# Weight conversion in words of 1024 columns, and w3 transposed by VectorE in 32x32 blocks

## The chip, the cores and the metric

The kernel runs on one core of one Trainium2 chip. The metric is the device time of one execution in microseconds (us). An execution takes 872.35 us (median of three, 871.92 to 874.18); the profiled one has a span of 870.7 us from its first to its last instruction. The engines are called TensorE (PE, with its weight loads as PEld), VectorE (DVE), ScalarE (ACT), GpSimd (POOL) and SyncE (SP, which here only issues transfers).

## The reference

An attention block with decay (RetNet, parallel form) is followed by a feed-forward block that multiplies two projections:

```python
scores = scale * np.matmul(q, k.transpose(0, 1, 3, 2))          # q, k, v: (8, 8, 576, 64) fp32
ret = scores * Dmat[None, :, :, :]                              # causal, gamma_h ** (i - j)
x = np.matmul(ret, v).transpose(0, 2, 1, 3).reshape(4608, 512)
a = x @ w1                                                      # w1, w2: 512 x 1024
b = x @ w2
h = a * b @ w3                                                  # w3: 1024 x 1024
out = h @ w_out                                                 # w_out: 1024 x 512
```

The four weight matrices come in as float64, q, k and v as float32; the output is float32, 4608 x 512. So the kernel has to make float32 words from the two 32-bit words of each float64, and it does so with integer and float instructions on the chip.

## The kernel before

**Folding of the last two products.** (a*b) @ w3 @ w_out is computed as (a*b) @ (w3 @ w_out). The small product w3 @ w_out (1024 x 512) is made once on TensorE, called the w3 stage here, and its result is kept in SBUF (`w3o`). For each of the 8 row blocks `ft` of w3 (128 rows), `w3_tr` (L433) transposes the 128 x 1024 block on TensorE in eight 128x128 pieces into PSUM (L438), ScalarE copies them to SBUF (L440) as `w3T`, and `w3_mm` (L443) multiplies the eight pieces with the eight row blocks of w_out into one PSUM bank (L448), which ScalarE copies to `w3o` (L451). A matmul in fp32 appears as two records in the trace.

**The up step.** `up(i, n, fp)` (L476) computes, for a block of tokens (i, n) and a quarter `fp` of the 1024 columns, both x @ w1 and x @ w2 in Strassen form: seven products of four matmuls each (L493) on TensorE, five additions on VectorE (`plus`, L498), two copies on ScalarE (L506, L513), and a last elementwise product a*b (L519). The Strassen sums of the weights (`strassen_weights`, L154, four VectorE instructions, L156) must be made before the ups of that `fp`, and the token sums (`strassen_tokens`, L458) before the ups of that block. `down` (L583) makes the product with `w3o`, also in Strassen form.

**The conversion.** `blocks` (L309) lists the pieces of the weights in the order of use: sixteen of w1 and w2 ("w12", fp, j, r), eight of w_out ("wo", g), and sixteen of w3 ("w3", ft, g0). Each is 128 x 512 float64, 512 KB. `load_block` (L319) issues the transfer of the next one on SyncE's queue, into one of five `raw` buffers. The conversion of a block is five VectorE and two ScalarE instructions:

- `begin_block` (L353): the exponent `e` from the high word (L362), the mantissa `m` from the high word (L366), the low word added to the mantissa (L369), and on ScalarE two ReLUs that clamp and shift the exponent (L372, L373);
- `end_block` (L378): the sign put into `e` (L383), the last reader of `raw`, and the final product m * e (L392), which writes to the place of use: `wA`, `wo`, or a row block `w3`. When a block is done, the next transfer is issued.

**What sets the order.** Instructions are issued in the order of the program text, and each engine takes its own in that order. The conversion is a generator that stops (yields) after each VectorE instruction, and `convert(n)` (L422) lets it go n steps. `plus` calls `convert(conv)` after each addition, so the steps of the conversion lie between the additions of the ups: `conv=2` with another two at the end of each up while w1 and w2 are converted, less after that. In the w3 stage a loop (L730) takes the six ups that are left one by one, transposes and multiplies w3 row blocks as they are ready, and calls `convert(10)` between row blocks once the ups are used up. A row block of w3 isn't finished before the one two ahead of it has been turned (`turned`, L387).

PSUM has seven banks in rotation for all products (`acc`). The memory on the right side of SBUF holds first the attention's buffers beside `raw`, and from L722 on `ab3`, `wst` (w3, w3T, wo) beside `raw`; when these are closed (L748, L760) it holds attention's buffers again, for the chunks of tokens from number `NC` on, whose transfers are then issued (L762).

The function that the change removes is this:

```python
    def w3_tr(ft):
        t = pools["wst"].tile([P, KF, P], F32, tag="w3T", name="w3T")
        for i in range(0, KF, NP):
            tp = acc.tile([P, NP, P], F32, tag="acc", name="tp")
            for n in range(NP):
                nc.tensor.transpose(tp[:, n, :], live["w3", ft][:, (i + n) * P:(i + n + 1) * P],
                                    ident)
            nc.scalar.copy(t[:, i:i + NP, :], tp)
        live["w3T", ft] = t
```

Of the kernel before, what the change touches and what calls it, by code (L numbers as in the profile page):

```python
# [8 lines left out]
F32 = mybir.dt.float32  # L9
I32 = mybir.dt.int32  # L10
U32 = mybir.dt.uint32
ALU = mybir.AluOpType
PSUM = bass.MemoryType.PSUM

# [24 lines left out]
def kernel(  # L39
# [13 lines left out]
    nc = tc.nc  # L53
# [5 lines left out]
    CV = 512  # L59
# [15 lines left out]
    QC = CV // 2  # L75
# [65 lines left out]

    halves = range(DF // CV)
    wA = [wp.tile([P, 2, KD, CV], F32, tag=f"wA{h}", name="wA") for h in halves]
# [10 lines left out]
    def strassen_weights(fp):  # L154
        def tt(out, in0, in1, op):
            nc.vector.tensor_tensor(out=A(fp, out), in0=A(fp, in0), in1=A(fp, in1), op=op)  # L156

        tt("S1", "A21", "A22", ALU.add)
        tt("S2", "S1", "A11", ALU.subtract)
        yield  # L160
        tt("S3", "A11", "A21", ALU.subtract)
        tt("S4", "A12", "S2", ALU.subtract)
        live["S", fp] = True
        yield

    BL = 32
# [142 lines left out]
    blocks = []  # L309
    for fp in range(NQ):  # L310
        for j, w in enumerate((moe_w1, moe_w2)):
            for r in range(2):
                blocks.append((("w12", fp, j, r), w))
    blocks += [(("wo", g), moe_w_out) for g in range(KF)]
    blocks += [(("w3", ft, g0), moe_w3) for ft in range(KF) for g0 in range(0, DF, CV)]
    at = {key: n for n, (key, _) in enumerate(blocks)}
    loaded, begun, converted, turned = [0], [0], [0], [0]

    def load_block():  # L319
        n = loaded[0]  # L320
        if n == len(blocks):
            return
        key, w = blocks[n]
        t = raw.tile([P, CV, 2], I32, tag="raw", name="raw", bufs=5)
        if key[0] == "w12":
            _, fp, _, r = key
            src = w[2 * r * P:2 * (r + 1) * P, fp * QC:(fp + 1) * QC, :]
            t2 = t.rearrange("p (c n) t -> p c n t", c=2)
            if r == 0:
                nc.sync.dma_start(t2, src.rearrange("(c p) n t -> p c n t", p=P))  # L330
            else:
                for half in range(2):
                    nc.sync.dma_start(t2[heads[half]],
                                      src.rearrange("(c a d) n t -> a d c n t", a=2, d=D)[1 - half])
        else:
            r, c0 = (key[1], 0) if key[0] == "wo" else key[1:]
            nc.sync.dma_start(t, w[r * P:(r + 1) * P, c0:c0 + CV, :])
        live["raw", n] = t
        loaded[0] += 1

    def converted_to(n):
        key, _ = blocks[n]
        if key[0] == "w12":
            _, fp, j, r = key
            return wA[fp // 2][:, j, 2 * r:2 * r + 2, fp % 2 * QC:fp % 2 * QC + QC]
        if key[0] == "wo":
            return live["wo"][:, key[1], :]
        _, ft, g0 = key
        if ("w3", ft) not in live:
            live["w3", ft] = pools["wst"].tile([P, DF], F32, tag="w3", name="w3")  # L350
        return live["w3", ft][:, g0:g0 + CV]

    def begin_block():  # L353
        n = begun[0]
        t = live["raw", n]
        lo, hi = t[:, :, 0], t[:, :, 1]
        e = raw.tile([P, CV], I32, tag="exp", name="e")
        m = raw.tile([P, CV], I32, tag="man", name="m")
        vec = nc.vector


        vec.tensor_scalar(out=e, in0=hi, scalar1=1, scalar2=21,  # L362
                          op0=ALU.logical_shift_left, op1=ALU.logical_shift_right)
        yield

        vec.tensor_scalar(out=m, in0=hi, scalar1=0x000FFFFF, scalar2=0x00100000,  # L366
                          op0=ALU.bitwise_and, op1=ALU.bitwise_or)
        yield
        vec.scalar_tensor_tensor(m.bitcast(F32), in0=lo.bitcast(U32), scalar=2.0 ** -32, in1=m,  # L369
                                 op0=ALU.mult, op1=ALU.add)  # L370
        relu = mybir.ActivationFunctionType.Relu
        nc.scalar.activation(e, e, relu, bias=lim[:, 0:1], scale=-1.0)  # L372
        nc.scalar.activation(e, e, relu, bias=lim[:, 1:2], scale=-2.0 ** 23)  # L373
        live["em", n] = e, m
        begun[0] += 1
        yield

    def end_block():  # L378
        n = converted[0]
        hi = live["raw", n][:, :, 1]  # L380
        e, m = live["em", n]
        vec = nc.vector
        vec.scalar_tensor_tensor(e, in0=hi, scalar=-(1 << 31), in1=e,  # L383
                                 op0=ALU.bitwise_and, op1=ALU.bitwise_or)
        yield
        key = blocks[n][0]
        while not (key[0] == "w12" or "wo" in live and (key[0] == "wo" or key[1] < turned[0] + 2)):  # L387
            yield "wait"
        out, m, e = converted_to(n), m.bitcast(F32), e.bitcast(F32)
        if key[0] == "w12":  # L390
            m, e = (x.rearrange("p (c n) -> p c n", c=2) for x in (m, e))
        vec.scalar_tensor_tensor(out, in0=m, scalar=2.0 ** -20, in1=e, op0=ALU.mult, op1=ALU.mult)  # L392
        converted[0] += 1

        if n >= 4:
            load_block()
        if key[0] == "w12" and key[1] > 0 and key[2:] == (1, 1):
            yield from strassen_weights(key[1])
        yield

    def conversion():


        yield from begin_block()
        while converted[0] < len(blocks):
            if begun[0] < len(blocks) and converted[0] not in (1, 2, 3):
                yield from begin_block()
            yield from end_block()
            if begun[0] == converted[0] < len(blocks):
                yield from begin_block()  # L410
# [11 lines left out]
    def convert(n):  # L422

        for _ in range(n):
            if go_on() is not None:
                return

    def convert_up_to(n):
        while converted[0] < n:
            assert go_on() is None  # L430


    def w3_tr(ft):  # L433
        t = pools["wst"].tile([P, KF, P], F32, tag="w3T", name="w3T")
        for i in range(0, KF, NP):
            tp = acc.tile([P, NP, P], F32, tag="acc", name="tp")
            for n in range(NP):
                nc.tensor.transpose(tp[:, n, :], live["w3", ft][:, (i + n) * P:(i + n + 1) * P],  # L438
                                    ident)
            nc.scalar.copy(t[:, i:i + NP, :], tp)  # L440
        live["w3T", ft] = t

    def w3_mm(ft, part):  # L443
        if part == 0:
            live["w3ps"] = acc.tile([P, DM], F32, tag="acc", name="ps")
        ps = live["w3ps"]
        for g in range(part * NP, part * NP + NP):
            nc.tensor.matmul(ps, live["w3T", ft][:, g, :], live["wo"][:, g, :],  # L448
                             start=(g == 0), stop=(g == KF - 1))
        if part == 1:  # L450
            nc.scalar.copy(live["w3o"][:, ft, :], ps)  # L451
# [24 lines left out]
    def up(i, n, fp, conv=0, tail=True):  # L476
# [43 lines left out]
        if tail:  # L520
            convert(conv)
# [142 lines left out]
    load_block()  # L664
# [8 lines left out]
    convert_up_to(3)  # L673
    load_block()
# [11 lines left out]
    up(0, 0, 0, conv=2, tail=False)  # L686
# [4 lines left out]
    convert(2)  # L691
# [4 lines left out]
    convert(5)  # L696
# [7 lines left out]
    up(0, 0, 1, conv=2)  # L704
# [5 lines left out]
    up(0, 1, 0, conv=2)  # L710
    pv(4)
    up(0, 1, 1, conv=2)
    up(0, 0, 2, conv=2)
# [11 lines left out]
    pools["forms"] = ctx.enter_context(tc.tile_pool(name="forms", bufs=1, reuse_waits="tile"))  # L725
# [3 lines left out]
    multiplied = 0  # L729
    while multiplied < KF:  # L730
        if todo:
            first = converted[0] < 4 * NQ
            up(*todo.pop(0), conv=2 if first else 1)
            convert(0 if first else 3)
        ft = multiplied
        begun_ft = ft < turned[0]
        if begun_ft:
            w3_mm(ft, 0)
        if turned[0] < KF and (not todo or converted[0] > at["w3", turned[0], DF - CV]):
            convert_up_to(at["w3", turned[0], DF - CV] + 1)  # L740
            w3_tr(turned[0])
            turned[0] += 1
        if begun_ft:
            w3_mm(ft, 1)
            multiplied += 1
        if not todo:
            convert(10)
# [3 lines left out]
    for nm in ("wB", "carry", "ot"):  # L751
        pools[nm] = ctx.enter_context(tc.tile_pool(name=nm, bufs=1, reuse_waits="tile"))
    xps.append(ctx.enter_context(tc.tile_pool(name="xp1", bufs=1, reuse_waits="tile")))
# [6 lines left out]
    weights_part.close()  # L760
    open_attention(ctx)
# [124 lines left out]
```

## Time and profile before

| what | value |
|---|---|
| time, median of three | 872.35 us |
| TensorE busy | 851.9 us, 98% of the span |
| VectorE busy | 458.3 us, 53% |
| ScalarE busy | 194.7 us, 22% |
| GpSimd busy | 111.8 us, 13% |
| up products on the chain that ended last (L493) | 46% |
| down products on it (L599) | 25% |
| w3 products on it (L448) | 6% |
| w3 transposes on it (L438) | 1% |

The busy share of an engine is an average over the whole span. TensorE's granted clock was full in nearly all of it. By stretches of the span, the busy times in us are:

| stretch, us | TensorE | VectorE | ScalarE | GB/s moved |
|---|---|---|---|---|
| 0 to 33.8 (first chunks, first weights) | 21.4 | 18.4 | 16.4 | 204 |
| 33.8 to 120.8 (ups with w1, w2 conversion) | 86.2 | 81.3 | 47.0 | 144 |
| 120.8 to 165.35 (ups with w_out, w3 conversion) | 43.2 | 39.8 | 17.9 | 107 |
| 165.35 to 222.7 (w3 stage) | 57.4 | 31.8 | 26.4 | 115 |
| 222.7 to 870.7 (all the rest) | 643.8 | 287.0 | 87.0 | 50 |

A group of instructions in the profile is shown as line, engine, operation, output <- inputs, shapes and count, then busy us and mean ns of one, then the idle time of the engine just before them and what ended it. A wait is shown as engine, what waited, what it waited for, and then us in total, times and the longest. The duration of one instruction includes a start that can overlap with the instruction before it; how far apart the starts lie is read from the timeline.

### The profile page before, as it was taken

What the parts mean: (1) busy time and instruction counts of PE and PEld (TensorE: products, weight loads), DVE (VectorE), ACT (ScalarE), POOL (GpSimd) and SP (SyncE); (2) the same over time, 40 slices, a digit from 0 to 9 for tenths busy, and PEclk for the clock granted to TensorE, in tenths of its full rate; (3) what the DMA queues carried; (4) which work ended last, traced back from release to release, by engine and by line L of the source; (5) the groups of instructions that cost most, each with busy time, mean ns of one, the idle gap of its engine ahead of it and who ended that gap; (6) DMA issues with size and microseconds to landing.
All of it is one profiled execution on the core that took longest, in us unless ns stands there. A gap on an engine that the chain in (4) does not pass through costs nothing.

```text
span 870.7 us, 15305 instructions
## 1 busy us (share of the span) xinstructions
PE 851.9 (98%) x6373; PEld 779.0 (89%) x6373; DVE 458.3 (53%) x781; ACT 194.7 (22%) x390; POOL 111.8 (13%) x91
## 2 busy tenths in 40 slices
PE   5899999999999999999999999999999999999998
PEld 5899999645888999999999999999999999999996
DVE  4799998973543344643544544534543434334343
ACT  3676333553022221101111101111101100001000
POOL 3000020002001323201212030230300101000000
PEclk9999999999999999999999999999999999999999
DMA  9993443437035444515242335061300000000001
GB/s 194 218 223 107 98 99 104 139 120 108 1 77 118 114 63 82 95 28 93 49 84 44 55 68 96 27 104 34 59 25 25 2 25 1 25 24 1 25 1 49
DMA packets 187332, 63.20 MB, mean 73 GB/s; under 512 B 175480, under 2 KB 175480, under 8 KB 187264
## 3 DMA queue, kind: packets, MB, share of 16 engines
q1 hardware_dynamic: 154624, 54.07, 29.2%
q10 hardware_dynamic: 32640, 8.16, 4.9%
q8 instruction: 50, 0.82, 0.4%
q14 instruction: 18, 0.15, 0.1%
HBM read 52.76 MB, written 9.44 MB: 71 GB/s over the span
## 4 chain that ended last, share of the span: by engine, by line
PE 88%; DVE 3%; issue 1%; DMA 1%; ACT 1%; DVEq 0%; ACTq 0%; SPq 0%
PE up L493 46%; PE po L599 25%; PE ps L448 6%; PE sc L241 4%; PE xps L298 3%; PE xps L291 2%; PE tp L226 1%; PE st L263 1%; DVE c L498 1%; PE tp L438 1%; DVE e L383 0%; DMA raw<-in_moe_w_dram 0%; ACT e L372 0%; DVE ab L519 0%; DVE w L392 0%
## 5 line engine op out<-in xcount | busy, mean ns | idle before, releaser
L498 DVE TENSOR_TENSOR c<-up,c 128x384 f32<-128x384 f32 x240 | 133.2, 555 | 198.0 <-PE up L493 193.2
L493 PE MATMUL up<-xT,wA 128*128 128x192 f32 x1152 | 213.5, 329 | 1.0 <-ACT xT L303 1.0
L493 PEld LDWEIGHTS up<-xT,wA 128*128 128x128 f32 x1152 | 191.9, 191 | 3.6 <-ACT xT L303 1.2
L493 PE MATMUL up<-T,wS 128*128 128x192 f32 x768 | 141.1, 327 | 2.1 <-DVE T L467 2.1
L493 PEld LDWEIGHTS up<-T,wS 128*128 128x128 f32 x768 | 127.8, 191 | 2.4 <-issue 2.4
L599 PE MATMUL po<-w3o,ab 128*128 128x256 f32 x456 | 104.2, 381 | 0.3 <-ACT ot L621 0.3
L599 PEld LDWEIGHTS po<-w3o,ab 128*128 128x128 f32 x456 | 86.0, 190 | 12.1 <-ACT ot L621 0.7
L603 DVE TENSOR_TENSOR ot<-po,ot 128x256 f32<-128x256 f32 x90 | 38.1, 424 | 72.3 <-PE po L599 70.6
L513 ACT COPY c<-up 128x384 f32<-128x384 f32 x48 | 22.9, 477 | 226.3 <-PE up L493 222.0
L493 PE MATMUL up<-xT,wS 128*128 128x192 f32 x384 | 70.6, 327 | 0.6 <-DVE c L498 0.5
L493 PE MATMUL up<-T,wA 128*128 128x192 f32 x384 | 70.3, 326 | 0.0
L244 DVE TENSOR_TENSOR pm<-sc,mask 128x512 f32<-128x512 f32 (+1 forms) x80 | 45.5, 628 | 46.7 <-PE sc L241 46.5
L599 PE MATMUL po<-wB,forms 128*128 128x256 f32 x288 | 65.1, 379 | 0.0
L493 PEld LDWEIGHTS up<-xT,wS 128*128 128x128 f32 x384 | 63.6, 190 | 1.5 <-DVE c L498 1.5
L493 PEld LDWEIGHTS up<-T,wA 128*128 128x128 f32 x384 | 63.7, 190 | 0.0
L599 PEld LDWEIGHTS po<-wB,forms 128*128 128x128 f32 x288 | 54.8, 190 | 7.3
L212 POOL TENSOR_TENSOR ld_v<-ld_v,gk 128x1024 f32<-128x1024 f32 (+1 forms) x17 | 32.3, 1900 | 213.6 <-DMA ld_v<-in_v_dram 186.3
L448 PE MATMUL ps<-wo,w3T 128*128 128x512 f32 x128 | 56.4, 593 | 0.2 <-ACT w3T L440 0.2
L506 ACT COPY c<-up 128x384 f32<-128x384 f32 x48 | 22.8, 476 | 117.4 <-PE up L493 68.4
L467 POOL TENSOR_TENSOR T<-xT,T 128x384 f32<-128x384 f32 x20 | 20.9, 1043 | 217.1 <-PE up L493 215.4
L519 DVE TENSOR_TENSOR ab<-c 128x768 f32<-128x768 f32 x48 | 46.6, 972 | 3.8
L448 PEld LDWEIGHTS ps<-wo,w3T 128*128 128x128 f32 x128 | 23.7, 190 | 27.2 <-issue 26.7
(75 smaller groups left out, 817.8 us busy)
## 6 DMA issues: line engine op xcount, KB each, us to landing
raw<-in_moe_w_dram SPq DMA_DIRECT2D x24, 512.0 KB, 3.7
out_dram<-ot SPq DMA_DIRECT2D x24, 256.0 KB, 2.0
bl_q<-in_q_dram SPq DMA_DIRECT2D x136, 32.0 KB, 2.1
bl_k<-in_k_dram SPq DMA_DIRECT2D x136, 32.0 KB, 2.2
raw<-in_moe_w_dram SPq DMA_DIRECT2D x16, 256.0 KB, 6.1
ld_k<-in_k_dram SPq DMA_DIRECT2D x8, 512.0 KB, 7.1
ld_q<-in_q_dram SPq DMA_DIRECT2D x8, 512.0 KB, 8.2
ld_v<-in_v_dram SPq DMA_DIRECT2D x8, 512.0 KB, 7.4
```

Of the source, the lines that this page charges most:

```text
L212: nc.gpsimd.tensor_tensor(out=t, in0=t, in1=gam[:sz, c].unsqueeze(1).unsqueeze(3).to_broadcast([sz, 2, H, D]), op=ALU.mult)
L241: nc.tensor.matmul(sc[j][:sz, p, :sz], kT[hs, b, p, :sz], qT[hs, b, p, :sz], start=True, stop=True)
L244: nc.vector.tensor_mul(pm[:sz, b, j, :, :sz], sc[j][:sz, :, :sz], mask[:sz, :sz].unsqueeze(1).to_broadcast([sz, NP, sz]))
L298: nc.tensor.matmul(banks[r][heads[half], b, n, :sz], vs[:sz, b * H + 2 * p + j, :], pm[:sz, b, j, p, :sz], start=(c == 0 and m == 0), stop ...
L448: nc.tensor.matmul(ps, live["w3T", ft][:, g, :], live["wo"][:, g, :], start=(g == 0), stop=(g == KF - 1))
L493: nc.tensor.matmul(ps[:, w, :], a[:, w, r, :], b[:, r, :], start=(new and w == r == 0), stop=(w == r == 1), skip_group_check=True)
L498: nc.vector.tensor_add(c[:, to], ps, c[:, sb])
L506: nc.scalar.copy(c[:, 0], p1)
L513: nc.scalar.copy(c[:, 0], p1)
L519: nc.vector.tensor_mul(ab[:, 4 * fp:4 * fp + 4, :], c[:, :, 0, :], c[:, :, 1, :])
L599: nc.tensor.matmul(ps[nm], a[A][:, f, :], live["W"][B][:, f, :], start=(f == 0 and not on), stop=(f == NP - 1), skip_group_check=True)
L603: nc.vector.tensor_add(ot[:, to[0], to[1]], ps[nm], ot[:, sb[0], sb[1]])
```

## The change

The conversion works on 1024 columns at a time: one item is two of the former blocks, a transfer of 1 MB in three buffers of twice the size, an exponent buffer of twice the width, and one mantissa buffer in place of two. The two first items (w1 and w2 of fp = 0) are still loaded and converted in halves of 512. The order of steps within an item changes: the exponent of the next item is begun between the mantissa of an item and its sign.

The rows of w3 are no longer transposed on TensorE. Four transfers bring 32-row blocks of a row block of w3 to four groups of 32 partitions, so that a VectorE transpose, which exchanges rows and columns within 32x32 blocks, gives the whole `w3T`. The inner dimension is then taken in another order (a, i, x), and w_out is loaded in the same order. It takes away `w3_tr`, the PSUM banks and the ScalarE copies of the transposes. `w3_mm` makes its eight matmuls in one go.

The pace of the conversion is set anew for items of double width (conv=1 where it was 2), and two pools are opened later: `forms` after the w3 stage, and `xp1` after the conversion's memory is closed.

```diff
-    CV = 512
+    CV = 1024
+    HC = CV // 2
...
+    blocks = [("w12", fp, j) for fp in range(NQ) for j in range(2)]
+    blocks += [("wo", g, 0) for g in range(0, KF, 2)]
+    blocks += [("w3", ft, 0) for ft in range(KF)]
+
+    items = []
+    for key in blocks:
+        items += [(key, h * HC, HC) for h in range(2)] if key[:2] == ("w12", 0) else [(key, 0, CV)]
...
-        t = raw.tile([P, CV, 2], I32, tag="raw", name="raw", bufs=5)
...
+            live["raw", key] = raw.tile([P, CV, 2], I32, tag="raw", name="raw", bufs=3)
...
+        elif kind == "wo":
+            src = moe_w_out.rearrange("(a i x) n t -> i a x n t", i=KF, x=BL)
+            t4 = t.rearrange("p (c n) t -> p c n t", c=2)
+            for c in range(2):
+                nc.sync.dma_start(t4[:, c], src[r + c])
         else:
-            r, c0 = (key[1], 0) if key[0] == "wo" else key[1:]
-            nc.sync.dma_start(t, w[r * P:(r + 1) * P, c0:c0 + CV, :])
-        live["raw", n] = t
+            src = moe_w3[r * P:(r + 1) * P].rearrange("(j r) (a f) t -> a r j f t", r=BL, f=FA)
+            t4 = t.rearrange("p (j f) t -> p j f t", f=FA)
+            for a in range(P // BL):
+                nc.sync.dma_start(t4[a * BL:(a + 1) * BL], src[a])
         loaded[0] += 1
...
+            live["m", key] = raw.tile([P, CV], I32, tag="man", name="m", bufs=1)
...
-        while not (key[0] == "w12" or "wo" in live and (key[0] == "wo" or key[1] < turned[0] + 2)):
+        while not (kind == "w12" or "wo" in live and (kind == "wo" or r < multiplied[0] + 2)):
             yield "wait"
...
+            flat = pools["wst"].tile([P, CV], F32, tag="w3", name="w3", bufs=1)
+            out = flat.rearrange("p (c n) -> p c n", n=QC)
...
+        if kind == "w3":
+            yield
+            t = pools["wst"].tile([P, KF, P], F32, tag="w3T", name="w3T")
+            vec.transpose(t.rearrange("p i (j r) -> p j i r", r=BL), flat)
+            live["w3T", r] = t
         converted[0] += 1
...
-        yield from begin_block()
-        while converted[0] < len(blocks):
-            if begun[0] < len(blocks) and converted[0] not in (1, 2, 3):
-                yield from begin_block()
-            yield from end_block()
-            if begun[0] == converted[0] < len(blocks):
-                yield from begin_block()
+        while converted[0] < len(items):
+            if begun[0] == converted[0]:
+                yield from begin_item()
+            yield from mantissas()
+            if converted[0] >= 4 and begun[0] < len(items):
+                yield from begin_item()
+            yield from end_item()
...
-    def w3_tr(ft):
-        t = pools["wst"].tile([P, KF, P], F32, tag="w3T", name="w3T")
-        for i in range(0, KF, NP):
-            tp = acc.tile([P, NP, P], F32, tag="acc", name="tp")
-            for n in range(NP):
-                nc.tensor.transpose(tp[:, n, :], live["w3", ft][:, (i + n) * P:(i + n + 1) * P],
-                                    ident)
-            nc.scalar.copy(t[:, i:i + NP, :], tp)
-        live["w3T", ft] = t
-
-    def w3_mm(ft, part):
-        if part == 0:
-            live["w3ps"] = acc.tile([P, DM], F32, tag="acc", name="ps")
-        ps = live["w3ps"]
-        for g in range(part * NP, part * NP + NP):
+    multiplied = [0]
+
+    def w3_mm(ft):
+        ps = acc.tile([P, DM], F32, tag="acc", name="ps")
+        for g in range(KF):
             nc.tensor.matmul(ps, live["w3T", ft][:, g, :], live["wo"][:, g, :],
                              start=(g == 0), stop=(g == KF - 1))
-        if part == 1:
-            nc.scalar.copy(live["w3o"][:, ft, :], ps)
+        nc.scalar.copy(live["w3o"][:, ft, :], ps)
+        multiplied[0] += 1
...
-    up(0, 0, 0, conv=2, tail=False)
+    up(0, 0, 0, conv=1)
     front(2)
     convert(1)
     scale(3, "q")
     front(3, "k")
-    convert(2)
     score(2)
     state(2)
     scale(3, "v", True)
     front(3, "q")
-    convert(5)
+    convert(3)
     pv(2)
...
-    up(0, 1, 1, conv=2)
-    up(0, 0, 2, conv=2)
+    up(0, 1, 1, conv=1, tail=1)
+    up(0, 0, 2, conv=1, tail=1)
...
-    while multiplied < KF:
+    while multiplied[0] < KF:
+        ft = multiplied[0]
         if todo:
-            first = converted[0] < 4 * NQ
-            up(*todo.pop(0), conv=2 if first else 1)
-            convert(0 if first else 3)
...
+            up(*todo.pop(0), conv=1, tail=converted[0] < at["wo", 0, 0])
+        else:
+            convert_up_to(at["w3", ft, 0] + 1)
+        if converted[0] > at["w3", ft, 0]:
+            w3_mm(ft)
+            convert(1 if todo else 6)
     w3_part.close()
...
-    for nm in ("wB", "carry", "ot"):
+    for nm in ("forms", "wB", "carry", "ot"):
         pools[nm] = ctx.enter_context(tc.tile_pool(name=nm, bufs=1, reuse_waits="tile"))
-    xps.append(ctx.enter_context(tc.tile_pool(name="xp1", bufs=1, reuse_waits="tile")))
...
     weights_part.close()
+    xps.append(ctx.enter_context(tc.tile_pool(name="xp1", bufs=1, reuse_waits="tile")))
     open_attention(ctx)
```

## The prediction

> **What bounds the kernel now.** I read the page's busy shares and slices first, then TensorE's waits, then the chain around the w3 stage, then the durations.
>
> ```profile
> PE 851.9 (98%) x6373; PEld 779.0 (89%) x6373; DVE 458.3 (53%) x781; ACT 194.7 (22%) x390; POOL 111.8 (13%) x91
> ...
> PE   5899999999999999999999999999999999999998
> ...
> DVE  4799998973543344643544544534543434334343
> ```
>
> A slice is 21.8 us. TensorE is the bound almost everywhere, so a microsecond of its work removed is a microsecond gained. VectorE is at 90% or more in slices 2 to 5 and again in slice 7, where the weights are converted: there it is a second limit just under the first. TensorE's waits on others (us in total, times, longest) show how close:
>
> ```profile
> PE up L493 <- DVE T L467: 2.1, 1, 2.1
> PE tp L438 <- DVE w L392: 1.1, 1, 1.1
> PE up L493 <- DVE c L498: 0.5, 1, 0.5
> PE ps L448 <- ACT w3T L440: 0.2, 1, 0.2
> ```
>
> The first ends at 33.8 us, in the start-up, and the change doesn't touch what it waits for. The others, with a short gap of about 0.2 us at 120.6, are 0.53 + 0.2 + 0.24 + 1.14 = 2.1 us that TensorE loses between 33.8 and 222.7 us because conversion is late. The chain of waits in order of time (start, us) at the w3 stage:
>
> ```profile
> 163.88 0.61 DVE e L383
> 164.51 0.70 DVE w L392
> 165.35 0.63 PE tp L438 x4
> 165.98 6.87 PE ps L448 x16
> 172.84 0.88 PE tp L438 x8
> 173.72 6.87 PE ps L448 x16
> 180.59 0.87 PE tp L438 x8
> ```
>
> From 165.4 to 222.7 us TensorE never pauses: each row block of w3 takes 6.87 us of products (an fp32 matmul is two records here, so x16 is 8 of them) and 0.875 us of eight transposes. Durations by form:
>
> ```profile
> L438 PE MATMUL tp<-ident,w 128*128 128x128 f32 x64 | 8.5, 273 | 1.1 <-DVE w L392 1.1
> L440 ACT COPY w3T<-tp 128x512 f32<-128x512 f32 x16 | 8.6, 587 | 5.9 <-PE tp L438 5.8
> L372 ACT ACTIVATE e<-e,lim 128x512 int32<-128x512 int32 x40 | 28.9, 723 | 44.3 <-DVE e L362 44.2
> L369 DVE SCALAR_TENSOR_TENSOR m<-raw,m 128x512 f32<-128x512 uint32 x40 | 27.6, 690 | 0.9
> L362 DVE TENSOR_SCALAR e<-raw 128x512 int32<-128x512 int32 x40 | 18.2, 456 | 4.1 <-DMA raw<-in_moe_w_dram 3.5
> L198 DVE STREAM_TRANSPOSE kT<-bl_k 128x1024 f32<-128x1024 f32 x8 | 9.9, 1239 | 0.0
> L536 DVE TENSOR_TENSOR w3o<-w3o 128x1024 f32<-128x1024 f32 x1 | 1.2, 1214 | 0.0
> ```
>
> 273 ns overstates what a transpose takes from TensorE, since neighbours overlap: eight pass in 0.875 us, 0.109 us each.
>
> [...]
>
> **The change, part by part.**
>
> *TensorE's transposes go.* 8 row blocks x 8 x 0.109 us = 7.0 us, all on TensorE's continuous path: -7.0.
>
> *VectorE transposes.* Eight 128x1024 at 1.24 us each (the L198 row) = 9.9 us added. Off TensorE's path if VectorE keeps up, which the next items examine. ScalarE loses 16 x 0.587 = 9.4 us of copies.
>
> *Words of 1024 instead of pairs of 512.* In the timeline, independent VectorE instructions start 0.33 us (TENSOR_SCALAR) and 0.60 us (SCALAR_TENSOR_TENSOR) after one another at 512; a dependent one waits for the full 0.69. The stream part doubles, the rest doesn't: 512 more elements add 0.53 us (1214 against 683 in the tensor_tensor rows) or half of it, 0.27. So 0.60 and 1.14 at 1024. A pair of blocks cost 2 x (2 x 0.33 + 3 x 0.60) = 4.9 us; a 1024-item costs 2 x 0.60 + 3 x 1.14 = 4.6. Eighteen such items save 5.4 us. Net for VectorE: +4.5 us over some 190 us.
>
> *The pace.* Before, an up step of 9.1 us on TensorE carries about 12 conversion steps: 12 x 0.49 + 5 additions x 0.47 + one product of 0.87 = 9.1 us of VectorE, equal to TensorE's, and anything extra (four Strassen sums, GpSimd beside it) makes it late. After, an up carries at most 6 steps. Following the generator by hand, the VectorE load of the ups from (0,0,1) on is 7.4 to 9.1 us each, mostly 7.8, and in the last, (0,2,2), the first w3 block's transpose is issued ahead of the last addition, some 0.2 us before the products want it. So the 2.1 us of lateness goes: -2.1.
>
> *One new wait at the second product.* In the order of issue, behind up(0,2,2)'s last matmul VectorE still has: addition 0.5, m 0.6, product 0.87, then for block 1 mantissa 1.2, next exponent 0.6, sign 1.14, final 1.22, transpose 1.24: 7.4 us, against 6.87 of w3_mm(0). TensorE waits 0.6; the ends are 0 (VectorE less behind) and 1.5 (every instruction at its dependent duration). I take +0.6.
>
> *The steady w3 stage.* VectorE needs 1.14 + 0.60 + 1.14 + 1.22 + 1.24 + 0.60 = 5.9 us per block, under 6.87. A longer loop runs through ScalarE: the ReLUs of block f+2 stand in its queue behind the copy of product f, which waits for TensorE. From the start of product f: 6.87 + copy 0.59 + two ReLUs + sign 1.22 + final 1.22 + transpose 1.24, to be ready when product f+2 starts, 13.74 later. No trace row has a 1024-wide ReLU: the lower end by slope (the trace's copies: 1048 ns at 1024, so about 0.43 per 512) is 1.16, the upper end twice 0.723 = 1.45. With 1.16 the sum is 13.5, hidden with 0.2 us to spare; with 1.45 and everything dependent 14.5, late by 0.8 every second block, 2.3 us in all. I take 0, as the wait at product 1 gives 0.6 us more room.
>
> *1 MB items in three buffers.* Where before an exponent step needed 512 KB, it needs 1 MB. In the first 70 us the transfers run at some 215 GB/s and limit. The item ("w12", 2, 0) is begun while (1,1) is still unfinished, so the sums of fp=1 stand behind it on VectorE. Its second half is the old block issued at 46.9 and 47.7 us, landing 6.2 to 6.5 us later: 54.1. By my count VectorE gets there at about 52. Then e 0.6, sign and final 2.3, S1 and S2 1.4 put S2 at 58.5, while TensorE wants it at 57.7 for the second product of up(0,0,1): +0.8, ends 0 and 1.8. The earlier items land in time: (1,1)'s last part at 41.5, wanted at 41.3. Later stages move 107 GB/s or so with a whole up of lead: hidden. The first 33.8 us keep their order, since the first four items stay 512 wide.
>
> *Placement.* forms and xp1 are opened later, raw grows by 4 KB and e/m by 4 KB in a partition. The last raw buffer comes free some 10 us before up(0,2,3) begins instead of 18, and the q/k/v loads that reuse it have more than 20 us until they are wanted: zero, hidden by up(0,2,3) and the first down.
>
> Sum: 872.35 - 7.0 - 2.1 + 0.6 + 0.8 = 864.7.
>
> **Rivals.** (1) *The ReLU loop or the product-1 wait is at its upper end*: +0.9 and +2.3 over the forecast, 867.9 with both. For: 0.2 us of room, and VectorE waits for ReLUs now (L383 sat idle 8.3 us for them). Against: ScalarE loses its w3T copies. (2) *Data late in the first 70 us*: +1.0 at S2 and a VectorE that stays late until up(0,1,0), which keeps the 0.5 and 0.2 us waits: 866.5; if the score and transposes of the next chunk are also late by 2 us, 868.5. For: transfers limit there. Against: VectorE has less to do in each later up. (3) *VectorE becomes the bound, slower*: beside GpSimd the trace shows exponents at 1.10 and signs at 1.02 instead of 0.42 and 0.69. If wide instructions ran at 1.4 times my price throughout, a w3 block takes 8.3 us instead of 6.87 (seven gaps, +10), and the ups at 10.2 instead of 9.1 add about 1.1 x 3: 864.7 + 13 = 878. Against: GpSimd is idle in the records between 130 and 200 us, and the 1024-wide rows at hand show no such price. (4) *The gain is eaten exactly*: 871 to 873, from (1) and (2) together with half of (3).
>
> **How the numbers follow.** Forecast 0.68; rival 1 0.12; rival 2 0.08; rival 3 0.07; rival 4 0.05. The low end is the forecast without both new waits and a little more: 864.7 - 0.6 - 0.8 - 0.7 = 862.6. The high end takes in (1) and (2): 869.5. Faster by over 0.3% means under 869.7: forecast, (1), nearly all of (2): 0.86. Within 0.3%: 0.07. Slower: 0.07.
>
> **What would show it.** Right: no tp line in the w3 stage; eight ps stretches at 6.87 us spacing but for a wait of about 0.6 us ahead of the second, on the VectorE transpose; up(0,2,3) starting near 215 instead of 222.7; TensorE's waits on c and w gone; a wait on wS of under 1 us near 58; VectorE's 1024-wide rows near 1.2 and 0.7, its transposes near 1.24, ReLUs near 1.16; after the w3 stage everything as before, only earlier. Wrong: ps spacing over 7.2 us with ScalarE's e or VectorE's transpose as what ends the wait; VectorE's load per up above 9.1; a wait on raw transfers of more than 2 us after 33 us; or a changed front before 33.8 us.

## The result and the profile after

The kernel became **slower**: 884.66 us (median of 4 runs, 884.39 to 885.97) against 872.84 us for the kernel before on the same chip (4 runs). The ratio is 1.0137, with an interval of 1.012 to 1.0155. The forecast was 864.7 with an upper end of 869.5, so both the sign and the range were wrong.

The page of the changed kernel begins as follows (busy time and share of each engine; then the span in 40 slices of 22.1 us, with TensorE's granted clock in tenths):

```profile
span 882.3 us, 15042 instructions
...
PE 849.8 (96%) x6309; PEld 773.9 (88%) x6309; DVE 460.3 (52%) x699; ACT 176.6 (20%) x338; POOL 112.4 (13%) x91
...
PE   5898995999999999999999999999999999999998
...
DVE  4896884898444333644544534444543424434243
...
PEclk9999998899999999999999999999999999999999
```

TensorE has 2.1 us less to do (851.9 before), although 7.0 us of transposes left it: the matmuls that remain took longer in places. It is idle for 882.3 - 849.8 = 32.5 us, before for 870.7 - 851.9 = 18.8. The holes are in slices 4 and 7, counted from one (about 66 to 88 and 132 to 154 us; the prediction counted its slices from zero), and in and after the second the clock falls too (mean over the span 0.990, before 0.998). The kernel isn't slower everywhere; it has two bad places. Four landmarks on TensorE divide the time (us):

| stretch | before | after | difference |
|---|---|---|---|
| start to up(0,1,1) | 84.58 | 90.43 | +5.85 |
| from there to the start of the w3 stage (its first transpose before, its first product after) | 74.2 | 86.3 | +12.1 |
| from there to up(0,2,3), the w3 stage | 63.94 | 56.70 | -7.2 |
| the rest | 647.97 | 648.84 | +0.9 |

The third row is the gain that was forecast. In the kernel before it counts from 158.8 us, where the first transposes begin; the earlier table counted the w3 stage from 165.35, the end of TensorE's last pause in it. The waits of TensorE in the first 250 us name the others (us in total, times, longest):

```profile
PE up L513 <- DVE c L518: 10.6, 2, 9.3
...
PE tp L227 <- POOL ld_q L213: 2.2, 2, 1.4
PE tp L227 <- ACT ld_q L211: 2.1, 3, 1.6
PE sc L242 <- ACT qT L230: 2.1, 1, 2.1
```

`c <- up` (L518) is the addition of an up, which frees a PSUM bank. It is not an expensive instruction (0.55 us), so the question is what stood ahead of it on VectorE. The chain of waits, 132 to 155 us (start, us), answers:

```profile
132.72 0.69 DVE e L369
133.41 0.33 SPq L349
...
133.78 18.10 DMA raw<-in_moe_w_out_dram
...
151.98 0.06 DVE e L369
...
152.59 0.55 DVE c L518
...
154.19 0.56 DVE c L518
```

The last item of w_out was on its way for **18.1 us**. VectorE had the exponent step `e` of this item (L369) at the head of its queue and waited 10.5 us for the data; the additions behind it could not pass. One of them reads the bank into which TensorE's next product adds, so TensorE waited too. Its timeline (start, us; in brackets the wait ahead of it) shows the price twice:

```profile
144.06 1.46 PE L513 MATMUL up<-xT,wA 128*128 128x192 f32 x8
154.79 2.93 PE L513 MATMUL up<-xT,wS 128*128 128x192 f32 x8 [9.27 <-DVE c L518]
157.51 2.35 PE L513 MATMUL up<-xT,wA 128*128 128x192 f32 x8
159.70 1.46 PE L513 MATMUL up<-T,wS 128*128 128x192 f32 x8
```

After 9.27 us of waiting the same eight records took 2.93 and 2.35 us, where they take 1.46 undisturbed: (2.93 - 1.46) + (2.35 - 1.46) = 2.4 us more. The granted clock was 0.50 from 150 to 158 us and 1.00 from 160 on. 9.3 + 2.4 is nearly the whole +12.1 of the second row.

**Why 18.1 us?** A window by window view (length, then busy time of TensorE, its loads, VectorE, ScalarE and GpSimd, granted clock, share of the 16 DMA engines in use, GB/s), first while only w_out is under way, then beside w3's first transfers (asked for from 135.0 us on), then with w_out alone again, and after TensorE's restart:

```profile
92.00:96.00 4.00, 4.00 (x27) 4.00 (x26) 2.36 (x5) 0.45 (x1) 0.00 (x0) 1.00 0.25 100
...
138.00:140.00 2.00, 2.00 (x14) 2.00 (x13) 2.00 (x3) 0.00 (x0) 0.00 (x0) 1.00 1.08 131
...
148.00:152.00 4.00, 0.00 (x0) 0.00 (x0) 0.02 (x1) 0.00 (x0) 0.00 (x0) 0.63 0.26 95
...
154.00:156.00 2.00, 1.21 (x4) 1.21 (x5) 2.00 (x4) 1.40 (x2) 0.00 (x0) 0.50 0.26 61
```

With w_out alone the share is 0.25, which is 4 of 16 engines, and 100 GB/s are moved. At that rate 1 MB takes 10.5 us (an estimate from this row); the rest of the 18.1 us went by while w3's transfers were under way beside it. In the kernel before, 512 KB of w_out landed in 3.5 us, 150 GB/s:

```profile
raw<-in_moe_w_out_dram SPq DMA_DIRECT2D x8, 512.0 KB, 3.5
```

The source of the changed transfer, `(a i x) n t -> i a x n t`, has a = 4 as its outermost dimension. In the kernel before it is the 128 rows, and with w_out alone under way from 92 to 96 us the share there is 0.54, with 177 GB/s moved. That the 4 is what holds the share at 0.25 is a reading of these two traces; experiments 1 and 4 test it.

**Why was it asked for so late?** The transfers' issues on SyncE's queue, of the changed kernel and then of the one before (start, time taken):

```profile
86.72 25.12 SPq L349 DMA_DIRECT2D raw<-in_moe_w_out_dram  x6
111.89 21.18 SPq L736 DMA_DIRECT2D gqs<-decay_q_dram  x16
133.18 1.14 SPq L349 DMA_DIRECT2D raw<-in_moe_w_out_dram  x2
```

```profile
102.54 10.51 SPq L721 DMA_DIRECT2D gqs<-decay_q_dram  x16
```

Sixteen small transfers (2.2 KB each) stand between the third item of w_out and the fourth. They took 21.18 us to issue behind the four-engine transfers, 10.51 before, and the last item of w_out was asked for only at 133.2. Small as they are, they keep the DMA engines in use: from 128 to 132 us the share was 0.60 with 4 GB/s moved. VectorE wanted the item at 141.5, 8.3 us after it was asked for. At the 150 GB/s of before, 1 MB would take 7.0 us (an estimate from the row above).

**The first row.** The chain of waits, 65 to 79 us, of the changed kernel:

```profile
65.93 0.61 DVE e L369
...
66.57 1.16 ACT e L372
...
67.75 1.15 ACT e L373
68.90 2.35 ACT ld_q L211 x8
...
71.29 1.33 PE tp L227 x5
72.62 1.70 PE xps L292 x32
...
78.20 1.82 PE up L513 x10
```

In the kernel before, ScalarE's timeline has a ReLU of half the width and the same scaling of q here (start, us, line):

```profile
61.90 0.72 ACT L372 ACTIVATE e<-e,lim 128x512 int32<-128x512 int32 x1 [3.49 <-DVE e L362]
...
63.43 2.46 ACT L210 ACTIVATE ld_q<-ld_q,gq 128x128 f32<-128x128 f32 x8
```

ScalarE's scaling of q for chunk 4 (L211), which the next transposes need, is put in its queue by hand after the fourth addition of up(0,0,1). Two ReLUs stand ahead of it in both kernels. Now each takes 1.15 us where it was 0.72, and their input, the exponent step on VectorE, comes 4.5 us later than before (65.93 against 61.45): the new order puts the mantissa steps of an item ahead of the next item's exponent, and up(0,0,1) itself begins 1.4 us later. So q is scaled from 68.9 us on instead of 63.4, and more of this comes from the late input than from the length of the ReLUs. TensorE waits 2.1 us and then runs at a lower clock (0.51 granted from 72 to 74 us): the 32 products of L292 take 1.70 us, in the kernel before 1.03. It reaches up(0,1,0) at 78.20, before at 72.36. An earlier wait of 2.1 us on qT, near 46 us, has the same form: copies behind ReLUs. It is where the 1.4 us at the start of up(0,0,1) come from, out of the row's 5.85.

**What was forecast and came.** The chain in the w3 stage has nothing left but products (a stretch of x64 is 4 row blocks), and the rows by form have the forecast durations:

```profile
184.38 27.96 PE ps L468 x64
...
219.46 14.00 PE ps L468 x32
233.46 2.61 PE up L513 x16
```

```profile
L390 DVE SCALAR_TENSOR_TENSOR m<-raw,m 128x1024 f32<-128x1024 uint32 x18 | 22.4, 1242 | 0.2
L372 ACT ACTIVATE e<-e,lim 128x1024 int32<-128x1024 int32 x18 | 20.7, 1150 | 38.5 <-DVE e L369 38.5
L369 DVE TENSOR_SCALAR e<-raw 128x1024 int32<-128x1024 int32 x18 | 12.5, 693 | 13.2 <-DMA raw<-in_moe_w_out_dram 10.5 <-DMA raw<-in_moe_w_dram 2.7
L420 DVE STREAM_TRANSPOSE w3T<-w 128x1024 f32<-128x1024 f32 x8 | 9.9, 1244 | 1.0 <-DVE w L416 0.5
```

The third row holds the cause in its last columns: of 13.2 us idle ahead of `e`, 10.5 were for w_out.

### The profile page after: what moved, and what is told of

Its sections match the earlier page's. It is cut to its first block, busy times and chain, and to the rows that moved or that the text cites. A ratio compares the mean times of both kernels' runs of the same rounds, so it can differ in the third digit from the quotient of the medians.

```text
span 882.3 us, 15042 instructions
## 1 busy us (share of the span) xinstructions
PE 849.8 (96%) x6309; PEld 773.9 (88%) x6309; DVE 460.3 (52%) x699; ACT 176.6 (20%) x338; POOL 112.4 (13%) x91
## 4 chain that ended last, share of the span: by engine, by line
PE 83%; DVE 6%; DMA 6%; issue 2%; ACT 1%; SPq 0%; POOL 0%; DVEq 0%; ACTq 0%; POOLq 0%
PE up L513 44%; PE po L618 24%; PE ps L468 5%; PE sc L242 3%; PE xps L299 3%; DMA raw<-in_moe_w_out_dram 2%; DMA raw<-in_moe_w_dram 2%; PE xps L292 2%; PE tp L227 1%; DVE c L518 1%; PE st L264 1%; DMA ld_q<-in_q_dram 1%; DMA ld_k<-in_k_dram 1%; DVE e L401 1%; DVE wS L159 1%
## 5 line engine op out<-in xcount | busy, mean ns | idle before, releaser
L518 DVE TENSOR_TENSOR c<-up,c 128x384 f32<-128x384 f32 x240 | 133.3, 555 | 190.8 <-PE up L513 183.3
L618 PEld LDWEIGHTS po<-w3o,ab 128*128 128x128 f32 x456 | 85.8, 190 | 13.2 <-DVE ab L584 0.9
```

Of the source, the lines that this page charges most:

```text
L518: nc.vector.tensor_add(c[:, to], ps, c[:, sb])
L618: nc.tensor.matmul(ps[nm], a[A][:, f, :], live["W"][B][:, f, :], start=(f == 0 and not on), stop=(f == NP - 1), skip_group_check=True)
```

## The experiments

The theory was: two independent losses, (A) w_out on four engines, asked for late, and (B) ScalarE's order in the first 90 us. Rivals were: words of 1024 make VectorE or ScalarE late everywhere; the order of SyncE alone is to blame; the w3 stage doesn't pay. Ratios are to the kernel before on the same chip, with intervals; diffs without another name are against the changed kernel.

**1. w_out in pieces of 32 partitions.** The data are the same, but each transfer has 32 as its outermost dimension.

```diff
             for c in range(2):
-                nc.sync.dma_start(t4[:, c], src[r + c])
+                for a in range(P // BL):
+                    nc.sync.dma_start(t4[a * BL:(a + 1) * BL, c], src[r + c][a])
```

> The changed kernel with each w_out transfer of 128 partitions split into four of 32 partitions; addresses and bytes are the same. Theory (the outermost dimension of 4 confines a w_out transfer to 4 of the 16 DMA engines): a 1 MB item lands in under 8 us instead of 18, TensorE's 9.3 us wait and the slow clock behind it go, 871 to 874 us. Rival (the scattered rows of w_out in memory are slow, or the transfers behind them are): landing stays near 18 us and the time near 884.7.

Measured: 873.14 us, ratio 1.0004 (0.9996 to 1.0013). The wait of 9.3 us on `c` is gone (1.3 remains, at 119 us), the sixteen small transfers take 8.56 us to issue, and in the window that follows the first issues the engines are in use three times as much:

```profile
88.00:92.00 4.00, 4.00 (x72) 3.43 (x71) 3.40 (x5) 1.57 (x4) 0.00 (x0) 1.00 0.78 200
```

The changed kernel has 0.27 and 78 GB/s there. The addresses are the same, so it was not where w_out's rows lie in memory; what differs is the outermost dimension of each transfer, 32 instead of 4. So (A) cost 1.3% of the time, nearly all of the loss.

**2. The small transfers later.** w_out stays on four engines, but the sixteen transfers of gqs are moved behind the w3 stage.

```diff
-    for a in range(2):
-        for f in range(D // BL):
...
     keep_stores.clear()
     store()
+    for a in range(2):
+        for f in range(D // BL):
...
```

> The changed kernel with the sixteen small gqs transfers issued after the w3 stage instead of ahead of the last w_out item. Theory (4 engines for w_out, and the queue that the gqs transfers hold up): the last w_out item is issued near 125.5 instead of 133.2 and lands near 143.7; VectorE's wait falls from 10.5 us to about 2, TensorE's from 9.3 to at most 1.5: 873 to 877 us. Rival (only the issue time matters, or only the rate): no wait at all and the same time as with the split transfers, or an unchanged 884.7.

Measured: 874.19 us, ratio 1.0016 (1.0007 to 1.0024). The last item of w_out is asked for at 126.7 us instead of 133.2, and VectorE's wait for it shrinks from 10.5 us to 1.9:

```profile
DVE e L369 <- DMA raw<-in_moe_w_out_dram: 1.9, 1, 1.9
```

TensorE's waits on `c` come to 2.0 us. Either repair is nearly enough: in the changed kernel the low rate did its harm only together with the late issue.

**3. Scaling q one addition earlier.** Only (B) is touched.

```diff
-    aside.extend([lambda: None] * 3 + [lambda: scale(4, "q", True)])
+    aside.extend([lambda: None] * 2 + [lambda: scale(4, "q", True)])
```

> The changed kernel with ScalarE's scaling of q of chunk 4 placed one addition earlier in up(0,0,1), ahead of the two wide ReLUs instead of behind them. Theory (ScalarE's order costs the first 90 us): TensorE's 2.1 us of waits on ld_q near 69 us and the slow clock after them go; up(0,1,0) starts near 74 instead of 78.1; the w_out wait stays, unless the later start shortens it: 880 to 882 us. Rival (q arrives late over the DMA, or VectorE is late): up(0,1,0) still starts near 78 and the time stays at 884.7.

Measured: 880.9 us, ratio 1.0094 (1.0074 to 1.0115). up(0,1,0) starts at 73.77 instead of 78.20, and up(0,1,1) at 86.00 instead of 90.43; the wait at w_out stays at 9.2 us. So the place of one instruction group in ScalarE's queue was worth 0.4%.

**4. The kernel before, with w_out on four engines.** This puts (A) into the kernel before, without any other part of the change. The rows of w_out are then paired with other columns of w3 than in the reference, so the folded product is another one; the work is the same.

```diff
-            r, c0 = (key[1], 0) if key[0] == "wo" else key[1:]
-            nc.sync.dma_start(t, w[r * P:(r + 1) * P, c0:c0 + CV, :])
+            if key[0] == "wo":
+                src = w.rearrange("(a i x) n t -> i a x n t", i=KF, x=32)[key[1]]
...
+            nc.sync.dma_start(t, src)
```

> The kernel before, with w_out alone loaded in rows (a, i, x) as in the change, 512 KB in one transfer with an outermost dimension of 4; rows of w_out are then paired with other columns of w3, so the folded product is not the reference's. Theory (4 engines): such a transfer takes some 9 us instead of 3.5, eight of them 72 us from 81.5 on, where 50 us are at hand: 885 to 895 us with waits on raw<-in_moe_w_out_dram. Rival (the rate of w_out matters only with 1 MB items and three buffers): 872 to 875.

Measured: 879.12 us, ratio 1.008 (1.0062 to 1.0098), less than expected. In the chain an item of 512 KB is on its way for 9.6 us, with two more items and the last of the small transfers asked for around it:

```profile
120.78 9.61 DMA raw<-in_moe_w_out_dram
```

TensorE waits 3.1 us instead of 9.3, then the clock is low (0.57 from 132 to 140 us). The expectation let eight transfers of 9 us follow one another, about half of the 18.1 us that 1 MB had taken beside w3's transfers. Where w_out alone is under way, from 92 to 104 us, the trace shows 86 to 103 GB/s at a share of 0.23 to 0.26; at that rate 512 KB take 5 to 6 us (an estimate). The access order therefore costs 6 to 7 us before the change, 11.6 after it.

**5. Experiments 1 and 3 together.**

> The changed kernel with both edits together: w_out in transfers of 32 partitions, and the scaling of q ahead of the wide ReLUs. Theory (two separate causes, the 16 engines and ScalarE's order): the gains add, 884.7 - 11.5 - 3.8 = 869.4, so 868 to 871. Rival (the same slack was spent twice): 872 to 873.

Measured: 867.96 us, ratio 0.994 (0.9925 to 0.9954). From 67 to 86 us the chain now has no hole (the wait on qT near 46 us stays):

```profile
67.43 1.75 PE tp L227 x16
...
74.10 9.30 PE up L514 x56
83.39 1.03 PE xps L292 x32
```

(1.33 + 0.43)% was the sum of the two alone, 1.97% is what both bring, so the two losses are independent to within the intervals, and repaired, the change is a gain.

**6. and 11. The pace of the conversion.** What remained in 5 was a wait of 1.8 us on qT, one of 1.3 on `c`, and 0.6 on wS. Experiment 6 moves conversion steps from the end of up(0,0,0) to a place behind front(2), and within up(0,1,2) from the first two additions to the third and fourth; 11 does only the first.

```diff
-    up(0, 0, 0, conv=1)
+    up(0, 0, 0, conv=[1, 1, 1, 0, 0])
...
+    convert(2)
     score(2)
...
-            up(*todo.pop(0), conv=1, tail=converted[0] < at["wo", 0, 0])
+            pace = [0, 0, 2, 2, 1] if len(todo) == 6 else 1
+            up(*todo.pop(0), conv=pace, tail=converted[0] < at["wo", 0, 0])
```

> As the one before, and the pace mended at two places: in up(0,0,0) the exponent step of the second 1 MB item comes after front(2), so that ScalarE makes c and the copies of kT and qT first; in up(0,1,2) the Strassen sums of fp = 3 come after the third addition, which frees the bank p5 that the seventh product writes. Theory: the 1.3 us wait of sc on qT and the 1.3 us wait of up on c go, with some slow clock behind the first: 865.5 to 868. Rival (VectorE's late data for the next item takes their place): 868 to 871.

> The kernel with w_out split, q scaled earlier and the exponent step of the second 1 MB item after front(2), but with the pace of up(0,1,2) left as in the change. Theory (the two edits of pace cancelled: the first took away the 1.8 us wait on qT, the second only moved the wait on c to the next up): 866.5 to 868.5, with a wait of 1.3 us on c near 117. Rival (neither matters): the same as without both, 868.

Measured: 868.08 us, ratio 0.9941 (0.9924 to 0.9958), and 867.69 us, ratio 0.9935 (0.992 to 0.995): no difference from experiment 5. The wait on qT went, and waits of 0.6 to 1.0 us on wA and of 1.8 in all on `c` were there in its place. With words of 1024, a step that is moved is moved whole.

**7. and 8. The transpose alone, words of 512 kept.** In 7 the kernel before transposes by VectorE at the place of `w3_tr`; w3 and w_out are loaded in pieces of 32 partitions. In 8 the transpose follows the second half of a row block at once, with the changed kernel's loop.

```diff
-        for i in range(0, KF, NP):
...
-            nc.scalar.copy(t[:, i:i + NP, :], tp)
+        nc.vector.transpose(t.rearrange("p i (j r) -> p j i r", r=32), live["w3", ft])
```

> The kernel before, with words of 512 as they were, and only the transposes changed: w3 and w_out by transfers of 32 partitions in the order (a, i, x), and one VectorE transpose of 128x1024 for each row block in place of eight on TensorE and two ScalarE copies. Theory (the transposes are worth what was forecast, and the width of 1024 is what costs): 7.0 us of transposes and the 0.24 us wait go, the 1.1 us wait may stay: 863.5 to 866. Rival (VectorE, which then does 9.9 us more without saving from wide words, is late in the ups): 867 to 873.

> As the kernel with the transposes alone (words of 512), with the VectorE transpose issued right behind the second half of its row block, as in the change, and not at the end of the ups. Theory (its 5.5 us wait before the first product and the slow clock behind it were a matter of where the transpose stood, so the transposes are worth some 8 us and the width of 1024 costs the rest): the wait becomes 0 to 1.5 us, 864 to 867. Rival (VectorE hasn't the time for the transposes without the saving of wide words): 868 to 872.

Measured: 871.82 us, ratio 0.9988 (0.9981 to 0.9995), and 869.48 us, ratio 0.9957 (0.9943 to 0.9972). In 7 the first row block makes TensorE wait, in 8 three of them do:

```profile
PE ps L449 <- DVE w3T L441: 5.5, 1, 5.5
```

```profile
PE ps L449 <- DVE w3T L402: 2.9, 3, 1.3
```

The changed kernel loses 0.7 us there. In 7 the clock is low after the wait (0.66 from 160 to 170 us), and the eight row blocks take 57.9 us instead of 55.0. In 8 the chain from 167 to 197 us goes round the loop that the prediction named: a product, ScalarE's copy of it, two ReLUs behind the copy, then VectorE's last steps and the transpose, and TensorE again. One round is 14.8 us for two row blocks, where their products alone take 13.7:

```profile
167.10:181.90 14.80, 13.97 (x32) 5.91 (x32) 13.24 (x23) 6.08 (x10) 0.00 (x0) 1.00 0.51 141
```

VectorE is busy for 13.24 of it and waits 1.0 for the ReLUs. In the changed kernel it is busy for 43.3 of 56 us there. So 7 us fewer on TensorE bring little unless VectorE has the room for the transposes, and the traces support that wide words give it that room. The totals do not show it: experiments 8 and 5 have intervals that overlap. Whether another pace would hide the loop with words of 512 was not tried.

**9. and 10. Early weights in halves, and w3 last.** Both start from experiment 5, with all of w1 and w2 converted in halves of 512 (at twice the number of steps), and only w_out and w3 in words of 1024. In 10, no product of the w3 stage is issued while ups are left to do.

```diff
-        items += [(key, h * HC, HC) for h in range(2)] if key[:2] == ("w12", 0) else [(key, 0, CV)]
+        items += [(key, h * HC, HC) for h in range(2)] if key[0] == "w12" else [(key, 0, CV)]
...
-    up(0, 0, 1, conv=1, tail=1)
+    up(0, 0, 1, conv=2, tail=2)
```

```diff
-        if converted[0] > at["w3", ft, 0]:
+        if not todo and converted[0] > at["w3", ft, 0]:
             w3_mm(ft)
-            convert(1 if todo else 6)
+            convert(6)
```

> The kernel with w_out split and the scaling of q earlier, and now all of w1 and w2 converted in halves of 512 with twice the steps, as before; w_out and w3 stay 1024 wide. Theory (in the first 100 us the wide ReLUs and the wait for 1 MB cost TensorE some 3 us): 864 to 866.5. Rival (width is harmless once ScalarE's order is mended): 867 to 869.

> The kernel with w1 and w2 in halves of 512, with the first w3 product held back until the six ups are used up, since in the run before it started among them and then waited twice, 3.8 us in all, for VectorE's transposes. Theory (that run lost its time in the w3 stage by pace, not in the first 100 us): both waits go and the time is 866 to 868.5. Rival (halves of 512 cost VectorE what wide words save, and it is late somewhere else): 869 to 874.

Measured for 9: 873.66 us, ratio 0.9998 (0.9985 to 1.0011). The first 100 us were in order (up(0,1,0) at 73.56), but w3 products came among the ups while VectorE was not ready for them:

```profile
PE ps L471 <- DVE w3T L421: 3.8, 2, 1.9
```

Measured for 10: **864.68 us, ratio 0.9902 (0.9885 to 0.9918), against 873.36 before**, the fastest of all. Its chain from 150 us on is TensorE alone:

```profile
149.88 9.43 PE up L516 x58
159.30 54.93 PE ps L471 x128
214.24 9.10 PE up L516 x56
```

54.93 us for eight row blocks is 6.87 each, the forecast pitch, without any pause. The margin over experiment 5 (3.3 us) was not divided by a run: the later w3 stage was not tried without the halves. In the two traces experiment 10 is 1.3 us ahead at up(0,1,1) (85.1 against 86.3) and gains another 1.6 in the w3 stage (54.9 against 56.5). Experiment 9, the same program up to there, reaches up(0,1,1) at 85.8, so part of the first difference is a difference between executions.

## Why the prediction was wrong

**The steps that failed.** First, "1 MB items in three buffers ... Later stages move 107 GB/s or so with a whole up of lead: hidden." The transfers were priced by the rate of the stage before, and their number of bytes was compared, not the form of the new source. With an outermost dimension of 4 the rate was 58 GB/s for the item that mattered, not 150, and 18.1 us met a lead of 8.3. Part of the lead was lost on SyncE, whose queue the working never went through: without the sixteen small transfers ahead of it (21.2 us) the item was asked for 6.4 us earlier. Experiments 1 and 2 show both halves; experiment 4 shows that the access order alone slows the kernel before. This is +11.6 us in experiment 1's terms, (1.0137 - 1.0004) x 873. It is also one of the prediction's own signs of being wrong, "a wait on raw transfers of more than 2 us after 33 us": VectorE's was 10.5.

Second, the same paragraph followed only VectorE and the transfers through the first 70 us. Its VectorE part came about as worked out: `e` waited for its data until 53.98 (forecast 54.1), and S2 cost 0.6 us in experiments 3 and 5 (forecast 0.8). What it left out is **ScalarE's order**: longer ReLUs, and above all later ones, ahead of q's scaling. ScalarE's queue was followed only in the w3 stage; experiment 3 shows +3.8 us for its order alone.

Third, "so the 2.1 us of lateness goes" rested on VectorE's load per up being below TensorE's 9.1 us. The load was so, but waits on additions remain, 1.3 us even in experiments 1 (at 119 us) and 5 (at 114 us), in an up where VectorE is busy for 8.1 of 9.3 us in experiment 5. In the program the seventh product of an up is added into the bank of the fourth (`p5`), so it waits for the third addition: TensorE may run ahead of VectorE by fewer than the seven banks. Ahead of that addition stood one final product of 1.22 us and four Strassen sums of some 0.6 us each, with two additions between them. That this reuse sets the slack is read from the program and from where the waits lie; no run changed it.

**The steps that held.** Transposes off TensorE and the steady w3 stage: -7.2 us measured for that stretch, against -7.0 - 1.4 (its part of the lateness) + 0.6 = -7.8. Wait at w3 products: 0.7 us in three pieces, forecast 0.6; only 0.3 of it lies at the second product, where the forecast had all, so the agreement of the sums is luck. ReLUs 1150 ns, forecast 1.16 us; transposes 1244 ns, forecast 1.24; `m` 1242 ns against 690 at 512, 0.55 us more, forecast 0.53; `e` 693 ns against 456, 0.24 more, forecast 0.27, and that this is half of the other was the author's estimate; the loop through ScalarE stayed hidden, as chosen (with words of 512, in experiment 8, it did not). Forecast and change minus the two overlooked losses nearly meet: experiment 5 is 4.8 us faster than before, the forecast was 7.7, and the waits that stay in it (qT 1.8, `c` 1.3) are of the size of the gap, though not every us of a wait ends up in the total. Experiment 10's time equals the forecast, but by other edits, and is no proof of it.

**The rivals.** "Data late in the first 70 us" named the right place but not ScalarE, and allowed 4 us where 5.85 were lost. "VectorE becomes the bound" had the right sign and the wrong cause: VectorE was waiting, not busy (4.0 of 4.0 us idle in the window from 148). Its premise was right in places: while GpSimd was at work, final products of 1024 took 1.56 us (at 126) and 2.93 (at 46) instead of 1.22. No case held a single late transfer with VectorE's whole queue behind it, though the additions lie between the conversion steps in that queue.

**What stays open.** The rest after up(0,2,3) is 0.9 us longer; a new wait of 0.5 us of TensorE for `ab` is in it, and the remaining 0.4 was not traced. Why the issue of small transfers takes longer behind those on four engines is not shown, nor what another order of banks in the up would do.

## What to carry to other kernels

When a transfer's source is reordered, look at its outermost dimension before its bytes: read the share of DMA engines in use in the windows where it runs alone, and if it has fallen, as here from 0.54 to 0.25 with 4 outermost, try the transfer in pieces with a larger number there (with 32, in experiment 1, the share was 0.78 and the time 1.3% less). For each wait that longer or fewer instructions could add, go through the queue of every engine, the issuing one and the one with a low share too, and write down what stands behind the instruction that waits. A coarser step saves time (an `m` of 1024 took 1242 ns, two of 512 before took 690 each) and takes away places to put it: here words of 1024 gave VectorE room in the w3 stage, and the fastest kernel had words of 512 among the hand-ordered ups, though how much of its gain they made was not shown.

## What the runs showed of the hardware

- Transfers of w_out with 4 as outermost dimension kept a share of 0.25 of the 16 DMA engines in use and moved 100 GB/s when alone (changed kernel, 92 to 96 us). With the 128 rows outermost it was 0.54 and 177 GB/s (before, the same window), with 32 it was 0.78 and 200 GB/s (experiment 1, 88 to 92 us). 1 MB with 4 outermost, asked for just before w3's transfers took 18.1 us, and 512 KB in experiment 4, with two more items around it, 9.6 us.
- Sixteen 2.2 KB transfers took 21.2 and, in experiment 4, 17.8 us to issue behind four-engine transfers on the same queue, 8.6 and 10.5 us behind spread ones (experiment 1, before).
- After a pause of 9.3 us TensorE took 2.93 us for eight records of 1.46 us, 2.35 for the next eight, and 1.46 again from some 5 us after the restart. After a pause of 3.1 us (experiment 4) the three groups of eight that followed took 2.92, 2.77 and 1.88 us; after one of 1.3 us (at 118 us in the changed kernel) 1.57 and 1.46.
